# Attention with a sketched kernel, then an MoE layer: a deeper MoE end with two sum banks, a new order, and warm matmuls up to the first wave

## The chip, the cores and the metric

The kernel runs on one core of a Trainium2 chip. Five engines work side by side and wait for each other through semaphores: PE (matmul, with its weight loads shown apart as PEld), DVE (vector), ACT (activation), POOL (GpSimd) and SP, which here only issues DMAs. Each runs its own instructions strictly in the order in which the program gives them, so the order in the source text is part of the design. The metric is device time in microseconds (us), the median of several runs. The profile comes from one execution, and its span is the time from the first to the last instruction.

## The reference

Four batches of attention, each with 4 heads, 1088 rows of 32 numbers. Rows of q and k are mapped to 64 features (an outer product of two projections to 8), then attention is linear. The result is the input of an MoE layer with 128 inputs, 2048 hidden units and 128 outputs over 4352 tokens.

```python
def phi(x):
    a = np.einsum('rd,bhsd->bhsr', S1, x)
    b = np.einsum('rd,bhsd->bhsr', S2, x)
    return np.einsum('bhsi,bhsj->bhsij', a, b).reshape(*x.shape[:-1], r * r)
q_p, k_p = (phi(q), phi(k))
kv = np.einsum('bhsf,bhsd->bhfd', k_p, v)
z = np.sum(k_p, axis=2)
num = np.einsum('bhsf,bhfd->bhsd', q_p, kv)
den = np.einsum('bhsf,bhf->bhs', q_p, z)[..., None] + 1e-06
attn_out = num / den
# ...
h = x @ w_in
g = h * (1.0 / (1.0 + np.exp(-beta * h)))
out = g @ w_out
```

## The kernel before

beta is folded into w_in (`winp`, scaled on POOL) and 1/beta into w_out (`woutp`, scaled on ACT), so that g is a plain silu. The tokens go through the MoE in ten chunks: two of 256, seven of 512 and a last one of 256. A chunk has eight **waves**. A wave is W1 (two matmuls of 512 columns, or four of 256, into a PSUM tile of two banks), one silu over 1024 columns on ACT, and later W2 (as many matmuls, added into the chunk's sum `moeout`). In the text below a token `W` issues the next W1 with its silu, if its tokens are ready, and `V` the oldest W2 that is not yet issued.

```python
psm = ctx.enter_context(tc.tile_pool(name="psm", bufs=2, space=PSUM))  # waves: 2 x 2 banks
pso = ctx.enter_context(tc.tile_pool(name="pso", bufs=1, space=PSUM))  # moeout, 1 bank
ps2 = ctx.enter_context(tc.tile_pool(name="ps2", bufs=1, space=PSUM))  # two(), 2 banks
ps1 = ctx.enter_context(tc.tile_pool(name="ps1", bufs=1, space=PSUM))  # one(), 1 bank
# ...
def w2(ci, j0, jn, g):
    t0, tw = tok_chk[ci]
    if j0 == 0:
        moe["acc"] = pso.tile([P, TCH], F32, tag="moeout", name="moeout")
    for jj in range(jn):
        j = j0 + jj
        nc.tensor.matmul(out=moe["acc"][:, :tw], lhsT=woutp[:, j, :], rhs=g[jj],
                         start=(j == 0), stop=(j == NJ - 1))
    if j0 + jn == NJ:
        o_sb = sbA.tile([P, TCH // 32, 32], F32, tag="o_sb", name="o_sb")
        nc.vector.transpose(out=o_sb[:, :nt, :]..., in_=moe["acc"][:, :tw])
        store(o_sb, ...)

def w1():
    # ...
    wv = psm.tile([P, 2, TCH], F32, tag="wave", name="wave")
    for jj in range(jn):
        nc.tensor.matmul(out=wv[...], lhsT=winp[...], rhs=xT[:, t0 : t0 + tw], start=True, stop=True)
    g = sbG.tile([P, 2, TCH], F16, tag="g", name="g")        # 6 buffers
    nc.scalar.activation(out=g[:, :, :gw], in_=wv[:, :, :gw], func=ACTF.Silu)
    moe["todo"].append(...)

def rest():                      # all that is left once the order below is through
    while moe["ci"] < len(tok_chk):
        if len(moe["todo"]) >= 2:
            second()             # W2
        w1()
    while moe["todo"]:
        second()
```

The front, up to the first wave, is the attention of the first 512 tokens of batch 0. It is written out by hand:

```python
kab(0)
rbeta_dve()
keep_warm(2)                     # matmuls of a constant tile that nobody reads
gram(0)
beta_half(0)                     # spreads beta over the partitions: 2 matmuls, 1 copy on ACT
outer(KP, 0, KAB, "kp", 0, 3)    # DVE: features of k, columns 0 to 3 of 9
gram_terms()                     # DVE
u = [wave2("bps") for _ in range(2)]
spread("b", 0, u)
KVZ[0] = pso.tile([P, TCH], F32, tag="moeout", name="kvz")
kv(0, range(0, 3))
gram_z()                         # PE, then a copy on ACT: z of batch 0
beta_half(1)
outer(KP, 0, KAB, "kp", 3, 6)
kv(0, range(3, 6))
mult(0, 0, u[0]); mult(0, 1, u[1])
outer(KP, 0, KAB, "kp", 6, 8)
outer(KP, 0, KAB, "kp", 8, 9)
gate(NJK - 1)                    # POOL waits here for the last outer
for c in range(0, 1024, 256):
    prep_win(c, c + 256)         # POOL
dps = one("dps"); den0(0, dps)
# ... eps, kv(0, range(6, 9)), kvd0 = copy of kv on ACT, 1/den spread on DVE (rbs)
ndps = two("ndps")[:, 0]
turn_nd(...)                     # PE transpose of kv
nc.scalar.copy(out=ND[0], in_=ndps[:, :P])
nps = wave2("nps")
num0(0, nps)
# ... the other winp on POOL, woutp 1 to 7 on ACT
for c in range(2):
    divide0(0, nps, rbs[c], c, c + 1)   # DVE: x of the first 512 tokens
turn_q(0, QA0, T)                # DVE: second part of q, batch 0

def a_B():
    PS["a"] = [wave2("aps"), two("aps")]
    spread("a", 1, PS["a"])
```

From there a string of tokens gives the order of everything, and `rest()` follows. Beside W and V: `aB bB c0 c1 mB dB iB nB xB` are the second part of batch 0 (projections, copies, products, den, 1/den, num, x); and for batches b = 1 to 3 `tk`/`tq` transpose k and q, `kp`/`qp` project, `ka`/`qa` transpose back, `o`/`p` are the outers of k and q (capital: DVE, small: POOL), `t` transposes of q's features, `gr gt gz gc gg gp` give z of batch 1 and `Z` that of batches 2 and 3 on DVE, `va`/`vb` are kv, `np`/`nz` its transpose, `d`/`i`/`n`/`x` den, 1/den, num and x; `w4` to `w7` scale two blocks of w_out on ACT; `lk lq lv` load. The string of the old kernel stands in the diff.

Of the kernel before, what the change touches and what calls it, by code (L numbers as in the profile page):

```python
# [9 lines left out]
F32 = mybir.dt.float32  # L10
# [4 lines left out]
P = 128  # L15
# [3 lines left out]
def kernel(  # L19
# [27 lines left out]
    TCH = 512  # L47
# [22 lines left out]
    pso = ctx.enter_context(tc.tile_pool(name="pso", bufs=1, space=bass.MemoryType.PSUM))  # L70
# [30 lines left out]
    for n, (s_, eng) in enumerate(((S1, nc.scalar), (S2, nc.gpsimd))):  # L101
        t = sb([P, D], F32, f"sr{n}")
        eng.dma_start(
            out=t, in_=bass.AP(tensor=s_.tensor, offset=s_.offset, ap=[[0, P // R], [D, R], [1, D]])
# [3 lines left out]
        out=bass.AP(  # L108
            tensor=beta4.tensor,
            offset=beta4.offset,  # L110
            ap=[[32 * beta4.ap[0][0], 4], [1, DFF // 4]],
        ),
        in_=moe_beta.rearrange("(r c) -> r c", r=4),
# [68 lines left out]
    def keep_warm(n, t=None):  # L182
        if t is None:
            t = pso.tile([P, TCH], F32, tag="moeout", name="warm")
        for _ in range(n):
            nc.tensor.matmul(out=t, lhsT=idle, rhs=cut(idle, [[0, 4], [1, P]]), start=True, stop=True)  # L186
# [14 lines left out]
    for c in range(4):  # L201
# [9 lines left out]
        out=mk,  # L211
# [13 lines left out]
    for n in range(2):  # L225
        t = sb([P, H, 2, 32], F32, f"zbg{n}")
# [18 lines left out]

    beta_bc = sb([P, DFF], F32, "beta_bc")

    def beta_half(i):
        t = two("betaps")
        for n in range(2):  # L250
            row = slice(64 * i + 32 * n, 64 * i + 32 * n + 32)
            nc.tensor.matmul(out=t[:, n], lhsT=ones[row, :], rhs=beta4[row, :], start=True, stop=True)  # L252
        nc.scalar.copy(
            out=beta_bc[:, 1024 * i : 1024 * i + 1024], in_=t.rearrange("p a b -> p (a b)")
        )

    winp = sb([P, DFF], F16, "winp")
# [32 lines left out]
    xT = sb([P, NTOK], F16, "xT")  # L290


    moe = {"ci": 0, "w": 0, "ready": 0, "acc": None, "todo": []}

    def store(o_sb, t0, u0, u1, queues):
        c = t0 + 32 * u0
# [15 lines left out]
    def w2(ci, j0, jn, g):  # L312
        t0, tw = tok_chk[ci]
        if j0 == 0:
            moe["acc"] = pso.tile([P, TCH], F32, tag="moeout", name="moeout")
        for jj in range(jn):
            j = j0 + jj
            assert j in scaled
            nc.tensor.matmul(  # L319
                out=moe["acc"][:, :tw],  # L320
                lhsT=woutp[:, j, :],
                rhs=g[jj],
                start=(j == 0),
                stop=(j == NJ - 1),
            )
        if j0 + jn == NJ:
            o_sb = sbA.tile([P, TCH // 32, 32], F32, tag="o_sb", name="o_sb")
            nt = tw // 32
            nc.vector.transpose(  # L329
                out=o_sb[:, :nt, :].rearrange("p t d -> p (t d)"), in_=moe["acc"][:, :tw]  # L330
            )
            last = ci == len(tok_chk) - 1
            store(o_sb, t0, 0, nt, [nc.sync, nc.scalar] if last else [nc.sync])
# [32 lines left out]
    def second():  # L366
        if moe["todo"]:
            w2(*moe["todo"].pop(0))

    def rest():  # L370
        while moe["ci"] < len(tok_chk):
            if len(moe["todo"]) >= 2:
                second()
            w1()
        while moe["todo"]:
            second()
# [14 lines left out]
    PS, KP, QO, QT, QP, ND, KAB, QAB, ASB, KVZ, KVD, RB = ({} for _ in range(12))  # L391

    def wave2(name):
        return psm.tile([P, 2, 512], F32, tag="wave", name=name)

    def two(name):
        return ps2.tile([P, 2, 512], F32, tag="two", name=name)

    def one(name):
        return ps1.tile([P, 512], F32, tag="one", name=name)  # L400
# [31 lines left out]
    def kab(b):  # L432
        KAB[b] = turn_ab(PS["kps"], "kab", [[8, NJK], [1, 8], [8 * NJK, 4]])
# [5 lines left out]
    def outer(dst, b, src, nm, j0, j1, eng=None):  # L439
        if b not in dst:  # L440
            dst[b] = sbA.tile([P, NJK, H, F], F32, tag=nm, name=nm, bufs=1)
        a0 = src[b][:, j0:j1]
        n = H * (j1 - j0)
        (eng or nc.vector).tensor_tensor(  # L444
            out=cut(dst[b][:, j0:j1], [[F, n], [R, R], [1, R]]),
            in0=cut(a0, [[2 * R, n], [1, R], [0, R]]),
            in1=cut(a0, [[2 * R, n], [0, R], [1, R]], R),
            op=MUL,
        )
# [11 lines left out]
    def spread(which, n, dsts):  # L461
        t0, tn = q_chk[n]
        for c in range(2):
            for m in range(2):
                for pr, dst in enumerate(dsts):
                    h = 2 * pr + m
                    rows = slice(32 * h, 32 * h + 32)
                    nc.tensor.matmul(  # L468
                        out=dst[64 * c : 64 * c + 64, m, : 32 * tn],
                        lhsT=(sa if which == "a" else sb_)[rows, :],  # L470
                        rhs=qT2[0][rows, t0 + c * tn : t0 + c * tn + tn, :],
                        start=True,
                        stop=True,
                    )
# [49 lines left out]
    def kv(b, j_list):  # L524
        for j in j_list:
            for h in range(H):
                nc.tensor.matmul(  # L527
                    out=KVZ[b][32 * h : 32 * h + 32, :F],
                    lhsT=v_t[b][:, h, j, :],
                    rhs=KP[b][:, j, h, :],  # L530
                    start=(j == 0),
                    stop=(j == NJK - 1),
                    skip_group_check=True,
                )
# [15 lines left out]
    def gram_terms():  # L550
        PS["zt"] = t = sbA.tile([P, H, R, R], F32, tag="zt", name="zt", bufs=1)
        nc.vector.tensor_tensor(
            out=t,
            in0=cut(PS["gram"], [[R, H], [0, R], [1, R]]),
            in1=cut(mk, [[R, H], [1, R], [0, R]]),
            op=MUL,
        )

    def gram_z():
        t = one("zc")  # L560
        for h in range(H):
            for c in range(2):
                nc.tensor.matmul(
                    out=t[64 * c : 64 * c + 64, 2 * h : 2 * h + 2],
                    lhsT=PS["zt"][:, h].rearrange("p i j -> p (i j)"),
                    rhs=e3[:, 1 - c : 3 - c],
                    start=True,
                    stop=True,
                )
        nc.scalar.copy(out=cut(zb0, [[32, H], [1, 2]]), in_=cut(t, [[2, H], [1, 2]]))  # L570
# [24 lines left out]
    def turn_nd(src, dst):  # L595
        nc.tensor.matmul(out=dst, lhsT=src, rhs=ident, is_transpose=True, start=True, stop=True)
# [32 lines left out]
    def num0(n, nps):  # L629
        w = 32 * q_chk[n][1]  # L630
        for h in range(H):
            for c in range(2):
                rows = slice(64 * c, 64 * c + 64)
                nc.tensor.matmul(
                    out=nps[32 * h : 32 * h + 32, c, :w],
                    lhsT=ND[0][rows, 32 * h : 32 * h + 32],
                    rhs=QP[n][rows, h % 2, h // 2, :w],
                    start=True,
                    stop=True,
                )  # L640
# [85 lines left out]
    asb(0, 1, w1_)  # L726
    rbeta_dve = prep_rbeta()
    kab(0)
    rbeta_dve()
    keep_warm(2)  # L730
    gram(0)
    beta_half(0)
    outer(KP, 0, KAB, "kp", 0, 3)
    gram_terms()
    u = [wave2("bps") for _ in range(2)]
    spread("b", 0, u)
    KVZ[0] = pso.tile([P, TCH], F32, tag="moeout", name="kvz")
    kv(0, range(0, 3))
    gram_z()
    beta_half(1)  # L740
    outer(KP, 0, KAB, "kp", 3, 6)
    kv(0, range(3, 6))
    mult(0, 0, u[0])
    mult(0, 1, u[1])
    outer(KP, 0, KAB, "kp", 6, 8)
# [12 lines left out]
    rbs = [spread_rc(rc, c, 8, 1) for c in range(2)]  # L758
    prep_wout_act(0)
    ndps = two("ndps")[:, 0]  # L760
    turn_nd(kvd0.rearrange("p c f -> p (c f)"), ndps[:, :P])
    ND[0] = sb([P, P], F32, "nd0")
    nc.scalar.copy(out=ND[0], in_=ndps[:, :P])
    nps = wave2("nps")
    num0(0, nps)
    for c in range(1024, DFF, 256):
        prep_win(c, c + 256)
    for j in range(1, NJ // 2):
# [5 lines left out]

    def a_B():
        PS["a"] = [wave2("aps"), two("aps")]
        spread("a", 1, PS["a"])

    def b_B():
# [65 lines left out]
    for b in range(1, B):  # L845
# [33 lines left out]
            DO[f"x{b}{i}"] = lambda b=b, i=i: divide_g(b, i, PS["nps"][i], RB[b][i])  # L879

    SEQ = """
        W aB c1 c0 bB tk1 w5 mB1 W mB0 kp1 w6 dB ka1 W o11 tq1 V W V qp1 w4 iB gr1 W qa1 w7 p11 W gt1 nB o10 W V V gz1 xB gc1 W V W O13 V gg1 p12 V O12 W gp1 V p13 W va1 vb1 W p10 V W t11 t12 np1 t13 t10 V W nz1 d1 W n1 V V tk2 V W i1 x10 kp2 x11 ka2 W V W lk3 V tq2 V W W O21 o22 V o23 O20 V V W W Z2 qp2 qa2 P20 va2 W W V P21 p23 V p22 V W V W V vb2 t20 W t21 t23 V t22 W lq3 V V np2 nz2 W W d2 tk3 lv3 i2 W V n2 x20 V V W x21 kp3 W V ka3 o32 W tq3 o33 V O31 W qp3 W O30 Z3 V V qa3 W W V p31 V V W W V va3 vb3 W P30 P33 V W t30 V np3 W nz3 V p32 W V W V t33 t32 t31 W V d3 W n3 i3 x30 W V x31 V
    """
    for s_ in SEQ.split():
        DO[s_]()
# [30 lines left out]
```

## Time and profile before

| what | value |
|---|---|
| time, median of 3 runs | 114.51 us (113.51 to 115.39) |
| span of the profiled execution | 113.1 us (that run took 115.1) |
| PE busy | 101.9 us, 90%, 1188 instructions |
| DVE busy | 73.0 us, 65%, 132 |
| ACT busy | 79.4 us, 70%, 100 |
| POOL busy | 28.9 us, 26%, 41 |
| first W1 starts | 16.24 us |
| last silu to the end of the span | 4.65 us |

A busy PE is not a PE at its peak: matmuls overlap, and their ends are modelled. So waits of PE are read from the starts of the matmuls, not from the busy share. The granted TensorE clock is listed for each stretch of time: 1.00 is full speed.

### The profile page before, as it was taken

The numbers are of one execution on the slowest core, as the hardware profiler recorded it, in microseconds if no ns is written. First come the engines' busy times: TensorE is split into PE (matmuls) and PEld (weight loads), VectorE is DVE, ScalarE is ACT, GpSimd is POOL, SyncE is SP. The second block draws the span as 40 slices with busy tenths as digits, with TensorE's granted clock in tenths as the row PEclk, the third lists the DMA queues.
The fourth block names the chain that finished last, engine by engine and source line by source line (L and its number), as shares of the span: only waits on it lengthen the run. The fifth ranks groups of instructions, "written<-read, shape, count | busy, mean of one in ns | idle before, by whom it ended". The sixth has DMA issues, their size and how long they took to land.

```text
span 113.1 us, 2913 instructions
## 1 busy us (share of the span) xinstructions
PE 101.9 (90%) x1188; PEld 48.3 (43%) x1188; DVE 73.0 (65%) x132; ACT 79.4 (70%) x100; POOL 28.9 (26%) x41
## 2 busy tenths in 40 slices
PE   6999958999999999999999999998998898799840
PEld 2335523256776443445454334464343333334520
DVE  5587795597199987999999989999396001000210
ACT  0634497547977953988979198997847889888830
POOL 5700378031990000801910053083000000000000
PEclk9999996569999999999999999999999999999999
DMA  3999999930030350041004954100400600140323
GB/s 80 342 275 251 375 362 380 378 139 0 6 46 13 51 185 3 0 74 25 0 15 73 232 179 74 19 6 12 68 13 0 91 7 0 28 67 0 52 41 46
DMA packets 24580, 11.33 MB, mean 100 GB/s; under 512 B 18900, under 2 KB 23028, under 8 KB 24568
## 3 DMA queue, kind: packets, MB, share of 16 engines
q1 hardware_dynamic: 23808, 11.05, 37.3%
q8 instruction: 9, 0.15, 0.6%
q10 hardware_dynamic: 696, 0.09, 0.5%
q14 instruction: 3, 0.02, 0.1%
q0 software_dynamic: 64, 0.02, 0.1%
HBM read 8.93 MB, written 2.23 MB: 99 GB/s over the span
## 4 chain that ended last, share of the span: by engine, by line
PE 68%; DVE 13%; ACT 8%; issue 4%; DMA 3%; DVEq 0%; ACTq 0%; POOLq 0%
PE moeout L319 21%; PE wave L344 20%; ACT g L353 7%; PE nps L690 4%; DVE o_sb L329 3%; PE kvz L527 3%; DMA sr<-in_S_dram 3%; PE dps L676 3%; PE kps L407 3%; PE betaps L252 2%; DVE kp L444 2%; DVE qT L386 2%; PE bps L468 2%; PE aps L468 2%; PE dps L602 1%
## 5 line engine op out<-in xcount | busy, mean ns | idle before, releaser
L353 ACT ACTIVATE g<-wave 128x1024 f16<-128x1024 f32 x68 | 66.4, 1021 | 19.3 <-PE wave L344 19.2
L319 PE MATMUL moeout<-g,woutp 128*128 128x512 f16 (+1 forms) x160 | 38.1, 347 | 3.8 <-ACT g L353 2.3
L344 PE MATMUL wave<-xT,winp 128*128 128x512 f16 (+1 forms) x160 | 40.4, 354 | 0.6 <-DVE xT L646 0.6
L319 PEld LDWEIGHTS <-woutp 128*128 128x128 f16 x160 | 15.1, 98 | 20.8 <-issue 7.0
L344 PEld LDWEIGHTS <-winp 128*128 128x128 f16 x160 | 14.6, 99 | 17.8 <-issue 7.1
L329 DVE STREAM_TRANSPOSE o_sb<-moeout 128x512 f32<-128x512 f32 (+1 forms) x10 | 6.3, 627 | 23.8 <-PE moeout L319 23.8
L444 POOL TENSOR_TENSOR qo<-qab 128x512 f32<-128x512 f32 (+1 forms) x8 | 12.0, 1523 | 12.9 <-DVE qab L429 12.9
L444 POOL TENSOR_TENSOR kp<-kab 128x512 f32<-128x512 f32 (+1 forms) x6 | 7.2, 1218 | 25.6 <-DVE kab L429 25.6
L444 DVE TENSOR_TENSOR kp<-kab 128x512 f32<-128x512 f32 (+2 forms) x10 | 9.8, 1016 | 0.0
L455 DVE STREAM_TRANSPOSE qt<-qo 128x512 f32<-128x512 f32 (+1 forms) x12 | 8.3, 739 | 0.0
L186 PE MATMUL warm<-idle 128*128 128x512 f16 x16 | 5.4, 490 | 1.1 <-DVE idle L98 1.1
L626 DVE STREAM_TRANSPOSE rb<-rc 128x576 f32<-128x576 f32 (+1 forms) x9 | 5.9, 685 | 0.2
L380 DVE STREAM_TRANSPOSE kT<-k 128x1088 f32<-128x1088 f32 (+2 forms) x5 | 5.3, 1061 | 0.7 <-DMA k<-in_k_dram 0.7
L527 PEld LDWEIGHTS kvz<-kp,v 128*32 128x32 f32 x288 | 4.4, 110 | 3.0 <-issue 1.7
L262 POOL TENSOR_TENSOR winp<-w_in_sb,beta_bc 128x256 f16<-128x256 f32 x8 | 5.6, 729 | 0.6 <-DMA w_in_sb<-in_moe_w_in_dram 0.6
L527 PE MATMUL kvz<-kp,v 128*32 128x64 f32 x288 | 5.4, 221 | 0.0
L277 ACT ACTIVATE woutp<-w_out_sb,rbeta 128x128 f16<-128x128 f32 x16 | 5.3, 395 | 0.0
L386 DVE STREAM_TRANSPOSE qT<-q 128x1088 f32<-128x1088 f32 (+2 forms) x5 | 5.2, 1049 | 0.0
L444 DVE TENSOR_TENSOR qo<-qab 128x512 f32<-128x512 f32 (+1 forms) x4 | 5.0, 1301 | 0.1
L690 PE MATMUL nps<-qt,nd 32*32 32x288 f32 x192 | 4.8, 413 | 0.0
L429 DVE STREAM_TRANSPOSE kab<-kps 128x288 f32<-128x288 f32 x8 | 3.4, 462 | 2.1 <-PE kps L407 2.1
L701 DVE TENSOR_TENSOR xT<-nps,rb 128x576 f16<-128x576 f32 x6 | 4.4, 738 | 0.3
(86 smaller groups left out, 75.5 us busy)
## 6 DMA issues: line engine op xcount, KB each, us to landing
v<-in_v_dram SPq DMA_DIRECT2D x15, 144.0 KB, 4.3
k<-in_k_dram SPq DMA_DIRECT2D x3, 544.0 KB, 6.3
q<-in_q_dram SPq DMA_DIRECT2D x3, 544.0 KB, 7.0
w_out_sb<-in_moe_w_out_dram SPq DMA_DIRECT2D x2, 512.0 KB, 7.6
w_in_sb<-in_moe_w_in_dram SPq DMA_DIRECT2D x2, 512.0 KB, 8.4
out_dram<-o_sb SPq DMA_DIRECT2D x16, 64.0 KB, 2.0
out_dram<-o_sb SPq DMA_DIRECT2D x10, 32.0 KB, 1.7
k<-in_k_dram SPq DMA_DIRECT2D x1, 288.0 KB, 2.9
```

The source lines that it names most:

```text
L186: nc.tensor.matmul(out=t, lhsT=idle, rhs=cut(idle, [[0, 4], [1, P]]), start=True, stop=True)
L262: (eng or nc.gpsimd).tensor_tensor(out=winp[:, c0:c1], in0=w_in_sb[:, c0:c1], in1=beta_bc[:, c0:c1], op=MUL)
L319: nc.tensor.matmul(out=moe["acc"][:, :tw], lhsT=woutp[:, j, :], rhs=g[jj], start=(j == 0), stop=(j == NJ - 1),)
L329: nc.vector.transpose(out=o_sb[:, :nt, :].rearrange("p t d -> p (t d)"), in_=moe["acc"][:, :tw])
L344: nc.tensor.matmul(out=wv[:, jj // per, o : o + tw], lhsT=winp[:, (j0 + jj) * P : (j0 + jj + 1) * P], rhs=xT[:, t0 : t0 + tw], start=True, ...
L353: nc.scalar.activation(out=g[:, :, :gw], in_=wv[:, :, :gw], func=ACTF.Silu)
L386: nc.vector.transpose(out=qT2[b % 2][:, t0:t1].rearrange("p t s -> p (t s)"), in_=q_t[b][:, t0:t1].rearrange("p t d -> p (t d)"),)
L444: (eng or nc.vector).tensor_tensor(out=cut(dst[b][:, j0:j1], [[F, n], [R, R], [1, R]]), in0=cut(a0, [[2 * R, n], [1, R], [0, R]]), in1=cut ...
L455: nc.vector.transpose(out=QT[b][:, j0:j1].rearrange("p j h c s -> p (j h c s)"), in_=QO[b][:, j0:j1].rearrange("p j h f -> p (j h f)"),)
L527: nc.tensor.matmul(out=KVZ[b][32 * h : 32 * h + 32, :F], lhsT=v_t[b][:, h, j, :], rhs=KP[b][:, j, h, :], start=(j == 0), stop=(j == NJK - ...
L626: nc.vector.transpose(out=rb, in_=cut(rc, [[1, n * tn], [0, 32]], i * tn))
L690: nc.tensor.matmul(out=tiles[g // 2][32 * h : 32 * h + 32, g % 2, :JW], lhsT=ND[b][rows, fc, 32 * h : 32 * h + 32], rhs=QT[b][rows, :, h, ...
```

## The change

It has three parts. **The MoE end**: in `rest()` W2 now stands three waves behind W1 and no longer two, and every other chunk's sum goes into the bank of `one()`, which attention no longer needs there; this is to take W2 off the path from one silu to the next, and the transpose of the finished sum out of the way of the next. **The order**: in the front, z and den of batch 0 and 1/den come ahead of the last outers as far as the data allow, the first beta matmuls take the place of two warm ones, and the token string is new. **Warm matmuls**: seven are added between the steps up to the second wave, where PE would wait for other engines, so that it stays active and its clock is not lowered.

```diff
-    def beta_half(i):
+    def beta_part(q0, q1):
         t = two("betaps")
-        for n in range(2):
-            row = slice(64 * i + 32 * n, 64 * i + 32 * n + 32)
+        for n, q in enumerate(range(q0, q1)):
+            row = slice(32 * q, 32 * q + 32)
 # ... (copies the same 1024 columns)
-            moe["acc"] = pso.tile([P, TCH], F32, tag="moeout", name="moeout")
+            alt = moe["alt"] and ci % 2
+            moe["acc"] = one("moeout") if alt else pso.tile([P, TCH], F32, tag="moeout", name="moeout")
 # ...
     def rest():
+        moe["alt"] = True
         while moe["ci"] < len(tok_chk):
-            if len(moe["todo"]) >= 2:
+            if len(moe["todo"]) >= 3:
                 second()
             w1()
 # ...
     kab(0)
+    beta_part(0, 2)
     rbeta_dve()
-    keep_warm(2)
     gram(0)
-    beta_half(0)
     outer(KP, 0, KAB, "kp", 0, 3)
-    gram_terms()
     u = [wave2("bps") for _ in range(2)]
     spread("b", 0, u)
     KVZ[0] = pso.tile([P, TCH], F32, tag="moeout", name="kvz")
     kv(0, range(0, 3))
+    outer(KP, 0, KAB, "kp", 3, 6)
+    gram_terms()
+    kv(0, range(3, 6))
     gram_z()
-    beta_half(1)
-    outer(KP, 0, KAB, "kp", 3, 6)
-    kv(0, range(3, 6))
+    beta_part(2, 4)
     mult(0, 0, u[0])
 # ...
     ndps = two("ndps")[:, 0]
+    keep_warm(1, ndps)
     turn_nd(kvd0.rearrange("p c f -> p (c f)"), ndps[:, :P])
     ND[0] = sb([P, P], F32, "nd0")
     nc.scalar.copy(out=ND[0], in_=ndps[:, :P])
     nps = wave2("nps")
+    keep_warm(2, nps[:, 0])
     num0(0, nps)
+    keep_warm(2)
 # ...
         PS["a"] = [wave2("aps"), two("aps")]
+        keep_warm(2, PS["a"][1][:, 0])
         spread("a", 1, PS["a"])
 # ...
-        W aB c1 c0 bB tk1 w5 mB1 W mB0 kp1 w6 dB ka1 W o11 tq1 V W V qp1 w4 iB gr1 W qa1 w7 p11 W gt1 nB o10 W V V gz1 xB gc1 W V W O13 V gg1 p12 V O12 W gp1 V p13 W va1 vb1 W p10 V W t11 t12 np1 t13 t10 V W nz1 d1 W n1 V V tk2 V W i1 x10 kp2 x11 ka2 W V W lk3 V tq2 V W W O21 o22 V o23 O20 V V W W Z2 qp2 qa2 P20 va2 W W V P21 p23 V p22 V W V W V vb2 t20 W t21 t23 V t22 W lq3 V V np2 nz2 W W d2 tk3 lv3 i2 W V n2 x20 V V W x21 kp3 W V ka3 o32 W tq3 o33 V O31 W qp3 W O30 Z3 V V qa3 W W V p31 V V W W V va3 vb3 W P30 P33 V W t30 V np3 W nz3 V p32 W V W V t33 t32 t31 W V d3 W n3 i3 x30 W V x31 V
+        tk1 W aB c1 c0 bB w5 W V mB1 kp1 mB0 w4 dB W ka1 V W w6 tq1 W o11 iB qp1 qa1 gr1 P11 gt1
+        w7 W V nB xB W p12 V gz1 W gc1 V V O13 gg1 o10 O12 W V gp1 W V W va1 vb1 p13 W p10 t12
+        V t13 np1 t11 V W t10 W V nz1 tk2 d1 V W n1 V i1 x10 W x11 V kp2 W ka2 W tq2 V V W qp2
+        O21 O20 W o23 V W o22 V V W W Z2 va2 qa2 p23 P20 V V W V W V P21 lk3 W t20 V p22 t21 vb2
+        t23 W V W t22 np2 V W nz2 V lq3 W d2 tk3 i2 W V n2 W V x20 x21 kp3 ka3 o32 W V tq3 lv3
+        W V O31 V o33 W qp3 W V W O30 V W Z3 qa3 V P33 p31 P30 V W V V W W V va3 t30 vb3 W V np3
+        W V p32 W t31 V nz3 t32 t33 W V W d3 W i3 n3 x30 W x31 V V V W V
```

A token stands at its place in the order of each engine that it uses; the engines themselves still run free of each other, up to their waits.

More of the change, by code (lines that the diff above doesn't have):

```diff
@@ L246 @@
     beta_bc = sb([P, DFF], F32, "beta_bc")
-    def beta_half(i):
+    def beta_part(q0, q1):
         t = two("betaps")
-        for n in range(2):
-            row = slice(64 * i + 32 * n, 64 * i + 32 * n + 32)
+        for n, q in enumerate(range(q0, q1)):
+            row = slice(32 * q, 32 * q + 32)
             nc.tensor.matmul(out=t[:, n], lhsT=ones[row, :], rhs=beta4[row, :], start=True, stop=True)
         nc.scalar.copy(
-            out=beta_bc[:, 1024 * i : 1024 * i + 1024], in_=t.rearrange("p a b -> p (a b)")
+            out=beta_bc[:, 512 * q0 : 512 * q1], in_=t[:, : q1 - q0].rearrange("p a b -> p (a b)")
         )
@@ L290 @@
     xT = sb([P, NTOK], F16, "xT")
-    moe = {"ci": 0, "w": 0, "ready": 0, "acc": None, "todo": []}
+    moe = {"ci": 0, "w": 0, "ready": 0, "acc": None, "alt": False, "todo": []}
     def store(o_sb, t0, u0, u1, queues):
```

## The prediction

> **What bounds the kernel now.** I read the page first (slices and groups), then the busy time in stretches around the one dip of the clock, then the timeline of the first 30 us, and last the chain that ended last, in its tail. From the page:
>
> ```profile
> PE   6999958999999999999999999998998898799840
> DVE  5587795597199987999999989999396001000210
> ACT  0634497547977953988979198997847889888830
> PEclk9999996569999999999999999999999999999999
> L353 ACT ACTIVATE g<-wave 128x1024 f16<-128x1024 f32 x68 | 66.4, 1021 | 19.3 <-PE wave L344 19.2
> L344 PE MATMUL wave<-xT,winp 128*128 128x512 f16 (+1 forms) x160 | 40.4, 354 | 0.6 <-DVE xT L646 0.6
> ```
>
> The kernel has three regimes. Up to about 16 us there is no wave of the MoE yet. From 16 to 84 us PE and DVE are both full. From about 87 us DVE is nearly empty and only the waves (W1, silu, W2) remain, with PE at 7 to 9 tenths and ACT at 8. ACT's 19.2 us of waiting for waves is the tail's and the slow stretch's, not a fault of ACT. The PEclk row has one dip, at slices 7 to 9; the busy times in stretches (stretch, length, busy us and instructions of PE, weight loads, DVE, ACT and POOL, then the granted clock, the DMA share and GB/s) place it:
>
> ```profile
> 17.00:17.50 0.50, 0.15 (x8) 0.18 (x15) 0.50 (x2) 0.50 (x1) 0.50 (x2) 1.00 1.15 385
> 18.00:18.50 0.50, 0.50 (x11) 0.23 (x2) 0.40 (x1) 0.00 (x0) 0.50 (x1) 0.50 1.08 386
> 24.00:24.50 0.50, 0.50 (x4) 0.38 (x3) 0.50 (x1) 0.00 (x0) 0.50 (x1) 0.50 0.31 108
> 24.50:25.00 0.50, 0.50 (x7) 0.42 (x5) 0.50 (x2) 0.24 (x1) 0.40 (x1) 0.97 0.09 30
> ```
>
> The stretch 17.5 to 18.0 has clock 0.70, so the clock fell at 17.7 and came back at 24.5: 6.8 us at half. The same projection of batch 1 and batch 2 in the timeline (start, duration) shows what that does to one instruction group:
>
> ```profile
> 21.49 1.22 PE L407 MATMUL kps<-kT,sk 64*32 64x288 f32 x16
> 43.85 0.72 PE L407 MATMUL kps<-kT,sk 64*32 64x288 f32 x16
> ```
>
> The same sixteen matmuls take 1.22 us at half clock and 0.72 at full. In the 3.4 us before the fall PE had little to do, because each step waits for another engine:
>
> ```profile
> 14.31 0.33 PE L596 MATMUL ndps<-ident,kvd 128*128 128x128 f32 x1 [0.39 <-ACT kvd L756]
> 14.99 0.67 PE L634 MATMUL nps<-qp,nd 64*32 64x256 f32 x16 [0.35 <-ACT nd L763]
> 16.24 0.60 PE L344 MATMUL wave<-xT,winp 128*128 128x256 f16 x4 [0.58 <-DVE xT L646]
> ```
>
> The tail repeats these five pieces of the chain (start, length, what):
>
> ```profile
> 98.62 0.04 issue
> 98.66 0.59 PE moeout L319 x2
> 99.25 0.45 PE wave L344 x2
> 99.74 0.04 issue
> 99.78 1.03 ACT g L353
> ```
>
> One turn is 1.03 + 0.04 + 0.59 + 0.45 + 0.04 + 0.04 = 2.19 us for two waves: silu i must end before W2 of i, PE runs strictly in order, so W1 of i+2 stands behind W2 of i, and silu i+2 behind that. ACT alone needs less: pairs of silus back to back take 1.94 us, triples 2.85, so 0.92 to 0.95 us from start to start.
>
> [...] half clock for 6.8 us, [...] after about 1.6 us of real matmul work in the 3.4 us before. [...] the tail runs with PE truly working 0.86 of every 1.10 us and stays at full clock[...]. [...] W2's first LDWEIGHTS starts at 97.98, before its matmul at 98.66, yet W1 behind it waits. [...]
>
> **The change, part by part.**
>
> Front, before the first wave. In the old order DVE does kp 0-3 (7.89), zt, kp 3-6, waits 0.43 for bps, then mult at 10.75. The new one drops two warm matmuls, puts the first beta matmuls (1.06) ahead of gram and moves zt behind kp 3-6, so bps runs at about 9.4 in place of 9.97 and mult starts at 9.74 (kp 3-6 done) + 0.42 (zt) = 10.16: 0.6 earlier, and kp ends 12.4. den0 then stands at 12.57 in place of 13.16, rb ends near 15.05. But ACT holds part of this back: the second beta copy (1.01) ends at about 13.6 and kvd0 behind it near 13.9, where it was 14.27. kvd0, ndps, nd, num0 take 1.75 (13.99 to 15.74), so num0 ends near 15.4 and the first wave is at about 15.85. Front: 0.4 us.
>
> Clock. Added: 1 + 2 + 2 + 2 = 7 warm matmuls of 0.216 at full clock (a pair of 512-column matmuls takes 0.43) = 1.5 us, set in the waits for kvd, nd, xT and the second qT. Work in the window before the fall rises from 1.6 to 3.1 of 3.4 us. They fill gaps of 0.68 (ndps to nps), 0.58 and 0.5, so they delay almost nothing (0.1). If the clock stays full, the stretch to the third wave becomes: aps 17.0-17.6 (qT is the limit), asb on ACT 17.6-18.8, bps to 18.95, second wave to 19.4, its neighbour W2 to 19.85, kps to 20.5, den0 to 21.1, third wave to 21.55. Before, the third wave ended at 24.73, with a W2 of 0.44 still to come: 25.17 against 21.55, so 3.6 us including the front's 0.4.
>
> Middle, third wave to num of batch 3 (82.39 before). PE sums: a wave or a W2 is 0.43, kps and qps 0.65, kv 1.13, ndps 0.22 or 0.44, dps 1.11, nps 1.53. Counted from the two orders, at num of batch 3 both have issued 47 waves, but 44 W2 before and 43 after; PE's load is the same to 0.4 us. DVE is the other bound: 14.39 of 16 us busy at 34 to 50 and 14.98 of 16 at 50 to 66, so one batch costs DVE about 21 us, as much as PE's 21.16 from one num to the next. The new order gives DVE one more outer (qo of batch 1, 1.3 us) and POOL one less. From 18 to 30 us DVE was busy 6.6 of 12 us (1.72 + 3.19 + 1.69 by four-us stretches); it now gets batch 1's kab at 20.5 in place of 22.8, so only 2.3 us earlier, and runs it nearly without idle: its pieces from kab to nd sum to about 14.3, so nd at 34.9 at best, 38.5 before. I let 0.2 us of the 3.6 be lost here: 3.4 us ahead at num of batch 3, so 79.0.
>
> Tail. After num of batch 3 (1.53) come one wave, three W2, a wave; the silu of that last wave starts 1.55 + 0.45 + 1.3 + 0.6 = 3.9 us after num's start. From there W2 is three waves behind, PE needs 0.86 per wave and ACT 0.95, so ACT is the bound and the first W2 of a chunk no longer waits for the transpose of the last sum (0.73 three times before, in part hidden). 20 silus x 0.95 = 19.0 to 19.4: last silu ends at about 79.0 + 3.9 + 19.2 = 102.1. Before: 108.46. After the last silu nothing changes: 113.1 - 108.46 = 4.65. Span 106.75, of which 2.95 is the tail and 3.4 all before it; sum 6.35 of 113.1.
>
> **The rivals.** (1) The clock falls anyway[...], or falls in another place: then only 0.4 + 2.95 less a delay by warm matmuls at half clock remain, about 3.2, a time of 111.4. For: [...] the old kernel's runs differ by 1.9 us (113.51 to 115.39)[...]. Against: after the change no 3.4 us window before 22 us has under about 0.8 of work. (2) DVE takes the place of PE in the middle: one outer more, and a batch already fills 15 of 16 us. Then the lead shrinks to 2.3 or 1.0 us by num of batch 3, time 110 to 111. Against: DVE idled in 18 to 30 us, so the outer has room. (3) The tail stays at 2.1 us per pair since PE at 0.86 and ACT at 0.95 are close and bubbles add up: 1 us less gain, 109.8. Against: triples in the old trace ran at 0.95.
>
> **Range and chances.** The profiled run took 115.1 for a span of 113.1, so 2.0 us lie outside it: 106.75 + 2.0 = 108.75; I predict 108.8. All gains at their best and a DVE chain without idle give 106.8; rival 1 or 2 with a normal tail gives 111.2. Faster by 2% means under 112.2, which needs two rivals together to miss: 0.91; within 2% 0.075; slower 0.015, which would take a new wait in the middle order that my count does not show.
>
> **What would show it.** PEclk at 9 in every slice; the third wave ending near 21.5; kps of batch 1 at 0.72 in place of 1.22; num of batch 3 near 79; ACT in the tail with idle under 0.1 us per wave and the chain there reading ACT g in place of PE moeout and wave; DVE's o_sb no longer releasing moeout. I would be wrong if PEclk still dips, if ACT waits for PE in the tail, or if DVE waits for POOL's outers in batch 1.

## The result and the profile after

The changed kernel takes 109.11 us (median; 109.02 to 109.26) against 114.01 for the kernel before beside it (112.98 to 115.39): a ratio of 0.960, 95% interval 0.952 to 0.968. Ratios here leave out executions over 1.5% above the fastest of their kernel, all of them with a mean clock of 0.983 or below. Predicted were 108.8 us, with 106.8 to 111.2 as the range.

The slices and the three large groups of the page after:

```profile
PE   6999998999999999999979999999999999999940
ACT  0707297979669863897978539989876799999920
PEclk9999999999999999999999999999999999999999
L354 ACT ACTIVATE g<-wave 128x1024 f16<-128x1024 f32 x68 | 65.7, 1038 | 14.8 <-PE wave L345 14.7
L345 PE MATMUL wave<-xT,winp 128*128 128x512 f16 (+1 forms) x160 | 40.1, 347 | 0.4 <-ACT g L354 0.2
```

The 68 silus are seven chunks of eight waves and three of four: a chunk of 256 tokens has four waves and not eight. The dip of the clock (0.50 from 17.7 to 24.5 us in the kernel before) is gone, ACT is at nine tenths in six slices near the end where it was mostly at eight, and its wait for waves fell from 19.2 to 14.7 us. The chain of waits in the tail (start, length, what) no longer passes through PE:

```profile
90.49 0.05 issue
90.54 0.87 ACT g L354
91.41 0.05 issue
91.46 0.87 ACT g L354
```

The timeline shows the marks that the prediction named. First num of batch 3 and one of the last pairs of silus in the kernel before:

```profile
82.39 1.60 PE L690 MATMUL nps<-qt,nd 32*32 32x288 f32 x64
...
99.78 1.94 ACT L353 ACTIVATE g<-wave 128x1024 f16<-128x1024 f32 x2 [0.26 <-PE wave L344]
```

Then the projection of batch 1, the third wave, num of batch 3, and the last twenty silus as one piece in the changed kernel:

```profile
20.56 0.72 PE L410 MATMUL kps<-kT,sk 64*32 64x288 f32 x16
...
21.85 0.61 PE L345 MATMUL wave<-xT,winp 128*128 128x256 f16 x4
...
80.19 1.60 PE L693 MATMUL nps<-qt,nd 32*32 32x288 f32 x64
...
84.19 18.44 ACT L354 ACTIVATE g<-wave 128x1024 f16<-128x1024 f32 x20 [0.74 <-PE wave L345]
```

Twenty silus in 18.44 us are (18.44 - 1.02) / 19 = 0.917 us from start to start, where two took 2.19 before. Num of batch 3 starts 2.2 us earlier (82.39 to 80.19), and from there to the end of the span it is 27.0 us in place of 30.7. So 3.7 of the 5.9 us lie in the tail and 2.2 before it. What the 2.2 are made of is less plain than it looks, and took the experiments.

Every run is read below at four marks: the first projection (kps of batch 0), the end of the third wave, the start of num of batch 3, and the end of the span. What lies before the third wave's end is called the front here, then comes the middle, and from num on the tail. The medians were taken in several sittings, in which the kernel before had 114.01, then 114.29 (for the first four experiments), 113.83 (the next three), 114.38 (the four from "after again" on) and 114.00 (the last).

| kernel | median us | first kps | third wave ends | num 3 | span | third wave to num | num to end |
|---|---|---|---|---|---|---|---|
| before | 114.01 | 5.86 | 24.73 | 82.39 | 113.1 | 57.66 | 30.7 |
| after | 109.11 | 5.89 | 22.46 | 80.19 | 107.2 | 57.73 | 27.0 |
| after, no added warm matmuls | 109.47 | 5.79 | 23.48 | 81.22 | 108.2 | 57.74 | 27.0 |
| before, warm matmuls added | 113.31 | 5.91 | 23.09 | 80.89 | 111.6 | 57.80 | 30.7 |
| before, new MoE end | 109.96 | 5.77 | 22.88 | 80.57 | 107.6 | 57.69 | 27.0 |
| after, old MoE end | 113.61 | 6.51 | 22.90 | 80.63 | 111.8 | 57.73 | 31.2 |
| after, three behind, one bank | 110.52 | 6.17 | 22.55 | 80.27 | 108.4 | 57.72 | 28.1 |
| after, two behind, two banks | 112.87 | 5.57 | 22.38 | 80.11 | 110.8 | 57.73 | 30.7 |
| after, old tokens | 109.48 | 6.23 | 22.61 | 80.30 | 107.4 | 57.69 | 27.1 |
| after again | 109.60 | 6.63 | 23.02 | 80.74 | 107.8 | 57.72 | 27.1 |
| one W2 moved | 108.66 | 6.72 | 23.25 | 80.41 | 107.4 | 57.16 | 27.0 |
| new start of the tail | 109.87 | 6.72 | 23.18 | 80.91 | 108.5 | 57.73 | 27.6 |
| both | 109.60 | 6.67 | 23.06 | 80.21 | 107.8 | 57.15 | 27.6 |
| freed wave buffer and moved W2 | 108.21 | 6.72 | 23.10 | 80.27 | 107.0 | 57.17 | 26.7 |

The first mark itself moves by over 1 us from run to run; the last section shows what moves it.

### The profile page after: what moved, and what is told of

It reads as the page before. It is cut to its first block, busy times and chain, and to the rows that moved or that the text cites. A ratio compares the mean times of both kernels' runs of the same rounds, so it can differ in the third digit from the quotient of the medians.

```text
span 107.2 us, 2923 instructions
## 1 busy us (share of the span) xinstructions
PE 99.7 (93%) x1193; PEld 48.3 (45%) x1193; DVE 74.3 (69%) x133; ACT 78.4 (73%) x100; POOL 28.6 (27%) x40
## 4 chain that ended last, share of the span: by engine, by line
PE 56%; ACT 20%; DVE 11%; DMA 4%; issue 4%; SPq 1%; DVEq 0%; ACTq 0%
ACT g L354 18%; PE wave L345 17%; PE moeout L320 15%; DMA q<-in_q_dram 4%; PE nps L693 4%; PE dps L679 3%; PE kvz L530 3%; DVE kp L447 2%; PE betaps L252 2%; DVE qT L389 2%; DVE o_sb L330 2%; PE bps L471 1%; PE aps L471 1%; PE kps L410 1%; PE gram L544 1%
## 5 line engine op out<-in xcount | busy, mean ns | idle before, releaser
L354 ACT ACTIVATE g<-wave 128x1024 f16<-128x1024 f32 x68 | 65.7, 1038 | 14.8 <-PE wave L345 14.7
L320 PE MATMUL moeout<-g,woutp 128*128 128x512 f16 (+1 forms) x160 | 38.9, 347 | 1.1 <-DVE o_sb L330 0.8
L447 POOL TENSOR_TENSOR qo<-qab 128x512 f32<-128x512 f32 (+1 forms) x7 | 11.5, 1658 | 11.9 <-DVE qab L432 11.9
L447 DVE TENSOR_TENSOR kp<-kab 128x512 f32<-128x512 f32 (+2 forms) x10 | 10.4, 1074 | 0.0
L186 PE MATMUL warm<-idle 128*128 128x512 f16 x16 | 5.9, 526 | 1.1 <-DVE idle L98 1.1
L447 DVE TENSOR_TENSOR qo<-qab 128x512 f32<-128x512 f32 (+1 forms) x5 | 5.7, 1179 | 0.1
L482 ACT COPY asb<-aps 128x512 f32<-128x512 f32 (+1 forms) x4 | 2.3, 616 | 3.5 <-PE aps L471 3.5
```

The costliest lines, as they stand in the source:

```text
L447: (eng or nc.vector).tensor_tensor(out=cut(dst[b][:, j0:j1], [[F, n], [R, R], [1, R]]), in0=cut(a0, [[2 * R, n], [1, R], [0, R]]), in1=cut ...
```

## The experiments

### Is the clock a part of its own?

The changed kernel without the seven warm matmuls:

```diff
-    keep_warm(1, ndps)
-    keep_warm(2, nps[:, 0])
     num0(0, nps)
-    keep_warm(2)
 # ... and in a_B
-        keep_warm(2, PS["a"][1][:, 0])
```

> The changed kernel without its seven added warm matmuls. Theory A (the clock is a part of its own, kept up by the warm matmuls alone): the clock falls to half between the first and the third wave, the third wave starts 2 to 3 us later than at 21.85, and the time is 111.3 to 112.0 against 109.1. Theory B (the new order of the front and of the tokens makes the lead, the warm matmuls only fill waits): the clock stays at 1.00 or its fall costs nothing because DVE has room, and the time is 108.9 to 109.4.

It took 109.47 us, but its four runs fall in two pairs: 108.61 and 108.83 at a mean clock of 1.00, and 110.11 and 110.18 at 0.979. The profile is one of the slower pair. Its clock is at half from 18.4 to 21.8 us, one stretch of 3.4 us, and its third wave starts 1.0 us later than in the changed kernel (22.87 against 21.85). So the event of theory A is there in two executions of four, at 1.4 us and not at its 2 to 3, and the other two are 0.1 to 0.3 us below the range of theory B. The median of the four is in neither range.

The converse, the kernel before with the seven added at the same places:

```diff
     ndps = two("ndps")[:, 0]
+    keep_warm(1, ndps)
 # ...
     nps = wave2("nps")
+    keep_warm(2, nps[:, 0])
     num0(0, nps)
+    keep_warm(2)
 # ... and in a_B
+        keep_warm(2, PS["a"][1][:, 0])
```

> The kernel before with the seven warm matmuls alone added at the same places. Theory A: no dip of the clock, kps of batch 1 at 0.72 us in place of 1.22, time 2.0 to 2.6 us under the kernel before. Theory B: within 0.5 us of the kernel before, since the old order has wider gaps and the clock falls or DVE holds the rest back.

It took 113.31 us (twenty runs, 113.07 to 114.17) against 114.29 for the kernel before, 1.0 us less. By the ratio, 0.996 (0.993 to 0.999), it is 0.5 us. Theory A is right about the clock and wrong about its worth; 0.5 us would be at the edge of theory B, but not for its reasons. The reason for both numbers is in the clocks of the 84 runs of the kernel before that stand beside all these experiments. By my estimate a stretch of 3.4 us at half clock, as in the profile of the first experiment, takes 3.4 / 2 / 113 = 0.015 off the mean of a run:

| mean granted clock | runs | mean us |
|---|---|---|
| about 0.97 | 14 | 115.40 |
| about 0.98 | 24 | 114.63 |
| 0.985 to 0.992 | 14 | 114.01 |
| above | 32 | 113.39 |

The upper row fits 6.8 us at half clock, as in the profile before (0.970), and the next one 3.4 us, as in that of the first experiment (0.979): by them the old kernel's clock falls in 38 of its 84 executions, and costs 1.2 or 2.0 us then; on the mean of the 84 these falls cost 0.7. Its profile happened to show 6.8 us at half clock, the dearest case. Of the 102 runs of kernels with the warm matmuls none had a mean clock below 0.987. What such a mean holds is seen in the profile of "after again", which has 0.989. Here are the clock's slices, first of the changed kernel without warm matmuls (0.979), then of "after again":

```profile
PEclk9999999599999999999999999999999999999998
```

```profile
PEclk9999999999999999999999999999999999999995
```

In the second the clock falls only in the last slice, behind the last matmul. So the third row of the table is likely no fall on the way either, and its 0.6 us may be a late start, which "after again" has too (first projection at 6.63); no profile of the old kernel with such a mean was taken. The warm matmuls do what they are for, but are worth about 1 us in the median. Where the clock stays up anyway they cost a little: from the first projection to num of batch 3 it is 74.8 us in the next experiment's profile, which has the old order without warm matmuls and no dip, and 75.0 with them, and the undipped runs of the first experiment are 0.3 to 0.5 us under the changed kernel.

That little work of PE does not by itself bring the dip is seen in the busy times of the stretch 13.9 to 17.3 us. First the kernel before, then the kernel of the next experiment, which has the same front:

```profile
13.90:17.30 3.40, 1.62 (x25) 1.00 1.08 366
```

```profile
13.90:17.30 3.40, 1.83 (x40) 1.00 1.08 366
```

PE is busy for about half of both (second number), and the second one did not dip:

```profile
18.00:20.00 2.00, 1.59 (x32) 0.51 (x19) 0.61 (x1) 1.54 (x5) 2.00 (x4) 1.00 1.08 381
20.00:22.00 2.00, 1.57 (x29) 0.58 (x28) 1.62 (x3) 1.76 (x5) 0.39 (x1) 1.00 1.03 393
```

In the changed kernel PE is busy 3.27 us of that stretch. This is not the stretch that ends at the fall: the 3.4 us before 17.7 hold 1.95 us of PE time in the kernel before, and those before 18.4 hold 1.94 in the changed kernel without warm matmuls. The least busy 3.4 us between 6 and 29 us hold 1.62 or 1.63 in these two and in the one that did not dip, 2.78 in the changed kernel and 2.47 or more in every profile with the warm matmuls; the ends of matmuls are modelled, so these are upper figures of the work. By its mean clocks the kernel before had the dip in 38 of 84 executions and not in the others; what decides between them is not shown.

### Is the MoE end a part of its own?

The kernel before with the new MoE end alone:

```diff
-            moe["acc"] = pso.tile([P, TCH], F32, tag="moeout", name="moeout")
+            alt = moe["alt"] and ci % 2
+            moe["acc"] = one("moeout") if alt else pso.tile([P, TCH], F32, tag="moeout", name="moeout")
 # ... in rest()
+        moe["alt"] = True
-            if len(moe["todo"]) >= 2:
+            if len(moe["todo"]) >= 3:
```

> The kernel before with the new MoE end alone (W2 three waves behind, sums in two banks). Theory A (the tail is a part of its own): silus back to back at 0.92 us from the 28th last on, time 3.0 to 3.6 us under the kernel before. Theory B (the tail is fast only because the new order hands it more waves): under 1.5 us.

It took 109.96 us, 4.3 under the kernel before in the median and 3.7 in the tail of its profile (30.7 to 27.0), where the last twenty silus run as in the changed kernel:

```profile
84.57 18.44 ACT L354 ACTIVATE g<-wave 128x1024 f16<-128x1024 f32 x20 [0.74 <-PE wave L345]
```

The changed kernel with these same lines undone:

> The changed kernel with the old MoE end (W2 two waves behind, one bank). Theory A: pairs of silus every 2.19 us again, time 3.0 to 3.6 us over the changed kernel, 112.1 to 112.7. Theory B: under 1.5 us over it.

It took 113.61 us: its tail is 31.2 us, 4.2 more than with the new end. The old end is slower here than in the kernel before since the new string leaves one W2 more for it (43 are issued before num of batch 3, not 44). Theory A holds both ways, with more than I had asked for: the MoE end alone takes the kernel before to within 0.9 us of the changed one.

Its two halves apart. W2 three waves behind, but one bank (the line that sets `moe["alt"]` taken out):

> The changed kernel with W2 three waves behind, but all sums in the one bank. Theory A (the depth makes the tail, the bank next to nothing): the first W2 of a chunk waits some 0.4 us for the transpose, but the silu after it has its wave already, so silus still run back to back and the time is 109.0 to 109.4. Theory B (the transpose between chunks counts): 0.7 us at each of three chunk ends, 110.5 to 111.3.

It took 110.52 us. My theory A fell: the bank is worth 1.1 us of the tail (28.1 against 27.0). Of this kernel's timeline, one end of a chunk:

```profile
93.06 0.59 PE L345 MATMUL wave<-xT,winp 128*128 128x512 f16 x2
...
93.20 0.72 DVE L330 STREAM_TRANSPOSE o_sb<-moeout 128x512 f32<-128x512 f32 x1 [6.97 <-PE moeout L320]
...
93.97 0.59 PE L320 MATMUL moeout<-g,woutp 128*128 128x512 f16 x2 [0.32 <-DVE o_sb L330]
...
94.40 0.59 PE L345 MATMUL wave<-xT,winp 128*128 128x512 f16 x2
...
95.09 2.85 ACT L354 ACTIVATE g<-wave 128x1024 f16<-128x1024 f32 x3 [0.25 <-PE wave L345]
```

The first W2 of the next chunk waits until 93.97 for the transpose, so the next wave starts 1.34 us after the last one in place of 0.92. With two wave buffers ACT has at most one finished wave in hand, and 0.25 us of its time are lost here; gaps of 0.25 to 0.27 stand at three places in this tail. Each also breaks the row of silus, which are 1.02 us long but start 0.917 apart, and so costs 0.36: three times make the 1.1. I had allowed for the wait of PE, and counted the wave in hand as full cover.

Two banks, but two waves behind:

```diff
-            if len(moe["todo"]) >= 3:
+            if len(moe["todo"]) >= 2:
```

> The changed kernel with the sums in two banks, but W2 two waves behind. Theory A: pairs of silus every 2.19 us, only the longer gaps at chunk ends gone (0.14 us, three times), 112.9 to 113.4, so nearly all of the old tail's 4.5 us are back. Theory B: 110.5 to 111.5.

It took 112.87 us, 0.03 below theory A's range: silus in pairs every 2.19 to 2.20 us, in the two lines of its timeline

```profile
94.19 1.94 ACT L354 ACTIVATE g<-wave 128x1024 f16<-128x1024 f32 x2 [0.26 <-PE wave L345]
96.38 1.94 ACT L354 ACTIVATE g<-wave 128x1024 f16<-128x1024 f32 x2 [0.26 <-PE wave L345]
```

On the tail of the changed kernel with the old end (31.2 us), the bank alone gives 0.5, the depth alone about 3, and both 4.2: the bank counts for more once the depth has taken the silu's own chain away.

### What is the new token string worth?

The changed kernel with the old string, front and end new:

> The changed kernel with the old string of tokens; front, warm matmuls and MoE end stay new. Theory A (the new token order gains nothing in the sum: it loses in the middle what it gains elsewhere): 108.8 to 109.5. Theory B (the new token order is needed to carry the lead of the front to the end): 110.0 to 110.8.

It took 109.48 us, with 57.69 us from the third wave's end to num of batch 3, where the new string takes 57.72 to 57.74 in seven profiles. Theory A holds: the new string gains nothing that can be seen. So the 2.2 us before num all lie in front of the third wave's end, and the table divides them: 24.73 to 23.09 with the warm matmuls alone is 1.6 for the clock, in the profile with 6.8 us at half clock, and 23.09 to 22.46 is 0.6 for the front; these last two start alike (5.91 and 5.89), and q comes alike.

Where the string loses is seen in the changed kernel's timeline. PE waits 0.77 us in the middle for a finished sum to leave its only bank; DVE has its transpose behind two outers and a transpose of features (with the old string the longest such wait is 0.43 us, at 75.5):

```profile
51.22 2.61 DVE L447 TENSOR_TENSOR qo<-qab 128x512 f32<-128x512 f32 x2
53.75 0.70 DVE L458 STREAM_TRANSPOSE qt<-qo 128x512 f32<-128x512 f32 x1
54.38 0.67 DVE L330 STREAM_TRANSPOSE o_sb<-moeout 128x512 f32<-128x512 f32 x1
...
55.10 0.59 PE L320 MATMUL moeout<-g,woutp 128*128 128x512 f16 x2 [0.77 <-DVE o_sb L330]
```

So one token was moved:

```diff
-        ... P21 lk3 W t20 V p22 t21 vb2
+        ... P21 lk3 W V t20 p22 t21 vb2
```

> The changed kernel with one token moved: the last W2 of a chunk stands ahead of the first feature transpose of batch 2 (W V t20 for W t20 V), so its sum's transpose no longer stands in DVE's queue behind a transpose that waits for POOL. Theory A (the middle lost its lead because PE waits 0.77 us at 54.4 for that sum): num of batch 3 starts 0.4 to 0.7 us earlier and the time is 108.4 to 108.8. Theory B (DVE is full there, so what it does first makes no difference): within 0.2 us of the changed kernel.

and the unchanged kernel ran beside it:

> The changed kernel unchanged, as the yardstick for the three beside it: 108.9 to 109.4.

109.60 us (108.81 to 109.98) for the changed kernel this time, 108.66 (108.29 to 109.37) with the token moved. The wait shrinks in the trace:

```profile
55.29 0.59 PE L320 MATMUL moeout<-g,woutp 128*128 128x512 f16 x2 [0.18 <-DVE o_sb L330]
```

and from the third wave's end to num it takes 57.16 us in place of 57.72. The two later kernels with this token moved have 57.15 and 57.17, and the one beside them without it 57.73: so 0.57 us are shown by the traces, and theory A holds. The runs of the two overlap, and the larger difference of their medians, 0.9, is not settled. POOL, which I had named as what held the feature transpose up, was not it: that transpose follows DVE's outers without a gap (51.22 + 2.61 = 53.83, and it starts at 53.75). What the moved token takes out of the way of the sum is the 0.63 us of the feature transpose itself.

### What starts the tail late?

ACT waits 0.74 us before the last twenty silus. The first try made x of batch 3's first half earlier and put two of three W2 behind the next wave:

```diff
-        RB[b] = [spread_rc(rc, 2 * i, NJK) for i in range(2)]
+        RB[b] = [spread_rc(rc, 2 * i, NJK) for i in range(1 if b == B - 1 else 2)]
+        PS["rc"] = rc
+    def j_g(b):                      # token j
+        RB[b].append(spread_rc(PS["rc"], 2, NJK))
 # ...
-        ... i3 n3 x30 W x31 V V V W V
+        ... i3 n3 x30 W V j3 x31 W V
```

> The changed kernel with a faster start of the tail: x of the first half of batch 3 comes ahead of the second half's 1/den spread on DVE, and one W2 in place of three stands before the next wave. Theory A (ACT is the bound from there on, so its 0.74 us wait before the last twenty silus goes straight into the end): 108.3 to 108.6. Theory B (PE with the W2 put off becomes the bound at 0.86 per wave): within 0.2 us of the changed kernel.

> Both of these in one kernel. Theory A: the two gains add, 107.7 to 108.2. Theory B: no better than the better one of the two.

109.87 and 109.60 us: both tails are 27.6 us in place of 27.0, so this is a loss of 0.6, though the front half of x was ready. In the first of the two, 0.4 of it lie before the end of the last silu (22.82 us after num's start against 22.44) and 0.2 behind it. Theory A fell in both. The timeline of the first names what the wave waits for:

```profile
84.22 0.59 PE L345 MATMUL wave<-xT,winp 128*128 128x512 f16 x2 [0.74 <-ACT g L354]
```

It is the silu of the wave before. There are two wave buffers, and half of num of batch 3 lies in the other. So the two W2 that I moved had stood in a wait that was there anyway, and now delay the wave after. The last run frees the buffer: x's first half is read from the half of num that lies in the wave buffer, and is made ahead of the next wave. The split and the moved W2 of batch 2 are kept:

```diff
-        PS["nps"] = [two("nps"), wave2("nps")]
+        PS["nps"] = [wave2("nps"), two("nps")] if b == B - 1 else [two("nps"), wave2("nps")]
 # ...
-        ... i3 n3 x30 W x31 V V V W V
+        ... i3 n3 x30 W V W j3 x31 V
```

> The moved W2 of batch 2, the split 1/den spread of batch 3, and now the half of num of batch 3 that is read first lies in the wave buffer, so that this buffer is free for the next wave as soon as that half of x is made; one W2 stands between the two waves. Theory C (the 0.74 us wait of ACT before the last twenty silus is a wait for a wave buffer: one held num, the other the wave whose silu had to end first; the number of W2 between the waves did not set it): silus run back to back from the first after num of batch 3 on, from num to the end of the span takes 26.2 to 26.5 us in place of 27.0, time 107.6 to 108.2. Theory D (it was x, made on DVE, that came too late): 27.0 or more, 108.5 to 109.5.

It took 108.21 us (107.91 to 108.99), a ratio of 0.950 (0.946 to 0.955) to the kernel before, the lowest of all here. The silus of its timeline:

```profile
82.51 1.94 ACT L354 ACTIVATE g<-wave 128x1024 f16<-128x1024 f32 x2 [1.05 <-PE wave L345]
84.71 17.52 ACT L354 ACTIVATE g<-wave 128x1024 f16<-128x1024 f32 x19 [0.27 <-PE wave L345]
```

The gap of 0.74 is gone and one of 0.27 has come one wave later, behind the two W2 that follow, so the silus are not back to back from the first on, as theory C had it. That the gap went now and not in the first try, which also had x early and one W2 between the waves, names the buffer as what the 0.74 us waited for. The tail is 26.7 us, short of the 26.2 to 26.5 of theory C, and theory D is out. Up to the end of the last silu it is 21.96 us in place of 22.44, so 0.5 less; behind it 0.2 us are lost again, and why is not shown. The kernel was not run beside the changed one, so its distance to that one rests on the two ratios, whose intervals overlap a little, and on the marks: 0.6 us less between the third wave and num, from the moved W2, and 0.3 after it.

## Why the prediction was right

The total was 0.3 us low (108.8 for 109.11), and the tail and the clock were named as what would carry it. Of the profiled spans 6.35 us were to go and 5.9 went; in the medians it is 4.9, for the profile of the kernel before has the longest fall of the clock, and most executions have a shorter one or none. By its own steps:

- **Front, 0.4 us.** The first wave came at 15.94 for a predicted 15.85 and 16.24 before: 0.3. But the load of q came 0.7 us later in this profile than in the one before (DVE's first transpose of q starts at 6.30 and at 5.63). Profiles in which it came at like times give 0.6 to 0.7: 16.46 (old front, q at 6.18) against 15.87 (new front, 6.22), and 16.62 (old front with warm matmuls, 6.34) against 15.94. So the front gave a little more than predicted, and that the first wave came so near to its mark is in part luck.
- **Clock, 3.2 of the 3.6 us up to the third wave.** That the clock stays up with the warm matmuls was right (no mean clock below 0.987 in 102 runs), the size of the gain was not. The third wave ended at 22.46 and not at 21.55. Counted as in the prediction, with the W2 of 0.44 that the old kernel has still to come at that point, 2.7 us were gained and not 3.6: 0.6 from the front, 0.44 from the W2, 1.6 from the clock. Over all executions the clock is worth still less, 2.0 in the executions with a mean clock of about 0.97 (115.40 against 113.39) and 0.7 on the mean. Two terms were mis-sized. I took 0.65 us, the time to issue the aps projection, as the time until its result is there; the copy on ACT starts at 18.15, 1.1 us after the projection's start at 17.05, for a single one of these matmuls takes some 0.4 us in the timeline. And not all of the slow stretch is PE's: the second bps starts at 19.25 in the kernel before and at 19.27 in the undipped run of the same order, since it waits for ACT's copy, and from there to the third wave's end it is 5.48 and 3.61 us, not double. The 1.6 us of work that I gave for the 3.4 us before the fall belong to 13.9 to 17.3; up to the fall at 17.7 it is 1.95.
- **Middle, 0.2 us lost.** I had num of batch 3 at 79.0; it was 80.19, and 0.9 of that difference was there at the third wave. Counted the same way, the middle lost 0.5 us and not 0.2. It has the wait of 0.77 us for a sum behind DVE's queue, and moving one token gave 0.57 back. I had seen that DVE was full there, and had put no price on what stands behind what in its queue. The lead at num, 2.2 us, is near the 2.3 of my rival 2, but most of what was missing was lost before the middle; the outer that this rival named, moved to DVE, was not tested alone.
- **Tail, 2.95 us.** It was 3.7. The term that was too small is the gain per silu: I took 0.95 us from start to start out of triples of 2.85 us, but that is 2.85 / 3, and the last silu is 1.02 long, so it is (2.85 - 1.02) / 2 = 0.915. Twenty in a row ran at 0.917, so the last silu ended 22.4 us after num's start and not 23.1. The bank, which the expectation of the run with one bank counted as next to nothing, turned out to be worth 1.1 of the tail once W2 stands three behind. **Rival 3**, bubbles in the tail, is out: the twenty silus stand in one piece.
- **Rival 1**, that the clock falls anyway, is out: none of the 102 runs with the warm matmuls has a mean clock below 0.987, and in "after again", the profile of theirs with the lowest (0.989), it falls only in the last slice. The old kernel's spread of 1.9 us, which I gave as this rival's support, is for the most part what the table of clocks shows (115.40 us at about 0.97, 113.39 in the last row).

So the lead at num, from the clock and the middle, was taken 1.2 us too large and the tail's gain 0.75 too small. That these partly cancelled is luck; without it the total would have been further off, though in the range.

## What to carry to other kernels

When two engines pass work back and forth in order, count how many items each has in hand: one more stage of lag took PE off the path between silus (2.19 us for two before, 0.917 for one after), and with it the cost of the single sum bank rose from 0.5 to 1.1 us. Before moving work out of a wait, look up which buffer the waiting instruction needs; the first try here moved a W2 that merely filled such a wait, and lost 0.6 us. And a profile with an event that not every execution has gives the size of that event, not its share of the median: look at the spread of the runs first.

## What was not expected of the hardware

The clock recorded at the start is not the whole truth. The record says 1.00 (from 1.06 to 7.00 us in both profiles shown here), yet the first warm matmuls of 512 columns start 0.43 us apart, twice what they take later, and go over to 0.22 at a time that differs from run to run. Their weight loads in the kernel before show the steps of 0.43, and from 4.03 on five loads in 0.98 us:

```profile
3.17 0.15 PEld L186 LDWEIGHTS <-idle 128*128 128x128 f16 x1 [0.28 <-issue]
3.60 0.15 PEld L186 LDWEIGHTS <-idle 128*128 128x128 f16 x1 [0.28 <-issue]
4.03 0.98 PEld L186 LDWEIGHTS <-idle 128*128 128x128 f16 x5 [0.27 <-issue]
```

The thirteen matmuls in the kernel before, and then in the last experiment's kernel, with the projection behind them:

```profile
1.06 4.44 PE L186 MATMUL warm<-idle 128*128 128x512 f16 x13 [1.06 <-DVE idle L98]
```

```profile
1.06 5.72 PE L186 MATMUL warm<-idle 128*128 128x512 f16 x13 [1.06 <-DVE idle L98]
6.72 0.72 PE L410 MATMUL kps<-kT,sk 64*32 64x288 f32 x16
```

Where the thirteen take 5.72 us, the first projection starts at 6.72, and at 5.57 where they take 4.50 (the run with two banks and two waves behind), so the warm matmuls themselves stand in its way; part of that is made up later, for where the first projection is early the front waits for the load of q (0.96 us in the changed kernel, first projection at 5.89), and where it is late DVE waits for the projection instead (0.71 us in the last experiment's kernel, first projection at 6.72). These two executions, with the same program up to there and mean clocks of 0.996 and 0.994, end the third wave at 22.38 and at 23.10, 0.7 us apart. And 1.6 us of PE time in the least busy 3.4 do not settle whether the clock falls: by its mean clocks the same program had no fall in 46 of 84 executions, one of about 3.4 us in 24 and 6.8 us in 14.
